# Output projection with features, not heads, on the column tiles, and a new memory made by cast and 32x32 transpose

## The chip, the cores and the metric

The kernel runs on one core of a Trainium2 chip. The metric is the device time of one execution in microseconds. The core has five engines that run side by side and wait for each other through semaphores: TensorE (PE, with its weight loads shown as PEld), VectorE (DVE), ScalarE (ACT), GpSimd (POOL) and SyncE (SP, which issues transfers here). SBUF and PSUM have 128 partitions; TensorE writes its results to PSUM.

## The reference

Two results are mixed with a gate per token. `a` is attention with a recurrent memory: the sequence of 2048 tokens is cut into 64 segments of 32, each segment is put behind 8 memory rows, all 40 rows go through 32-head attention (mask, softmax, output projection Wo), the first 8 output rows become the memory of the next segment, the other 32 are output. `b` is layer norm, a two-layer MLP with gelu, and biases.

```python
for s in range(n_seg):                       # 64, one after the other
    h = concat([mem, x[:, 32*s:32*s+32]])    # 8 + 32 rows of 512
    q, k, v = h @ Wq, h @ Wk, h @ Wv         # 512 -> 32 heads x 128
    p = softmax(where(mask, q k^T * scale, -1e9))
    o = einsum('bhqk,bhke->bhqe', p, v)
    o = einsum('bhte,hed->btd', o, Wo)       # 32 heads x 128 -> 512
    mem = o[:, :8]                           # used by the next segment
    outs.append(o[:, 8:])
out = g * concat(outs) + (1 - g) * mlp(layernorm(x))
```

All inputs and the output are bf16.

## The kernel before, in words

The first 96 us are the MLP (its result goes to a DRAM buffer `c_dr`) with the loading of the attention weights; then comes the loop over 64 segments (`for s in range(nseg)`), about 10.2 us each, and a short end. The four segments `si` = 0 to 3 of a tile T of 128 tokens belong together. The order of all instructions is the order of the code (a manual schedule).

PE works with column tiles throughout: a matmul takes 128 rows (contraction), 32 columns of weights (32 query rows of the activations as weights) and a moving operand of up to 512 columns; `tile_position=(0, 32*c)` puts it on one of four column tiles, whose results land on partitions 32c to 32c+31. Four such matmuls, one per column tile, run at the same time; a group of four is called a set below. Each matmul has a weight load of its own.

The 40 rows of a segment are not computed together. 32 rows (24 of the new tokens and the 8 memory rows) go through the segment itself: `hT` holds them transposed (feature on the partition, 4 chunks `kc` of 128 features, 32 rows, of which the first RIDE=24 are tokens and the last 8 memory). The other 8 tokens of each of four segments (LEFT=8) are gathered into a 32-row group of the whole tile, and their projections do not depend on the memory. They are the fill: a generator `side(T, si)` gives 8 units of one set each (projections of the left rows of the next tile for si = 0, 1, 3; `wo_left`, the output projection of the left rows, for si = 2), and `run(n)` puts n units into PE's stream at chosen places. WS holds these numbers.

One segment in order: q and k (16 sets each of 512 columns, L122), transposes to QT and KT, scores in two halves (L259, L263), exp on ACT, v (L141), the sums (L270, L273, L616) and their reciprocals, `run(W1)`, attention times v (`av`: L283 and L288, two halves, the second of which needs the second normalization L710), casts to UT on ACT (L746), `run(W2)`, then the output projection.

`wo_pass` (function at L645) does the output projection of UT into the bank W. `wo_group` gives column tile c the heads i = 4*ih + c, so each column tile adds up other heads, over all 512 features; W then holds four partial sums, on partitions 32c + row. There are 8 sets of 512 columns. ACT casts W to `w` (L650, three pieces). `new_mem` (three calls) multiplies w with a selection matrix SelM (a 1 at 32c + m for each c), which adds up the four partial sums, transposes and picks the memory rows at once: 4 matmuls of 8 columns for a chunk of 128 features, 16 in all (L659). DVE casts the results to hT of the next segment (L661). A unit of fill stands between these steps. Only then can PE start q and k of the next segment.

The other output rows are picked in `out_sel` once per tile (L223, L227): SelR and SelL are matrices with a 1 for each of the four partial sums, again one set of 512 columns per matrix. In the loop it stands behind `wo_pass` of si = 0 (from T = 2 on). After the loop there are two more `wo_pass`, the rest of a `wo_left`, and the end (L805 to L818).

Of the kernel before, what the change touches and what calls it, by code (L numbers as in the profile page):

```python
# [27 lines left out]
def kernel(ctx, tc, A_x, A_mem0, A_Wq, A_Wk, A_Wv, A_Wo, A_seg_len, B_x, B_w1, B_b1, B_w2, B_b2, gate_w, out):  # L28
# [42 lines left out]
    hT = [ep.tile([P, KC, 32], BF16, name=f"hT{i}") for i in range(3)]  # L71
# [4 lines left out]
    MkF = ep.tile([P, 4 * EW + NG + 2 * M], BF16)  # L76
    Mk = MkF[:, 0:4 * EW].rearrange("p (a c) -> p a c", c=EW)
    BO = ep.tile([P, P], BF16)
    SelM = ep.tile([P, M], BF16)
    SelR = ep.tile([P, 32], BF16)  # L80
    SelL = ep.tile([P, P], BF16)
    SelI = ep.tile([P, 32], BF16)
# [36 lines left out]
    def qk_unit(bk, G, t, hf, kc):  # L119
        h0, h1 = HF[hf]  # L120
        for j in range(4):
            nc.tensor.matmul(bk[32 * j:32 * j + 32, :], lhsT=G[:, kc, :], rhs=W5[t][:, kc, h0:h1, j, :],  # L122
                             start=(kc == 0), stop=(kc == KC - 1), tile_position=(0, 32 * j))
# [15 lines left out]
    def v_unit(bk, G, vb, kc):  # L139
        for j in range(4):  # L140
            nc.tensor.matmul(bk[32 * j:32 * j + 32, :], lhsT=G[:, kc, :], rhs=Wv5[:, kc, 4 * vb:4 * vb + 4, j, :],  # L141
                             start=(kc == 0), stop=(kc == KC - 1), tile_position=(0, 32 * j))
# [4 lines left out]
    HORD = [(j, ih) for j in (0, 2, 1, 3) for ih in range(2)]  # L147

    def wo_group(bk, U_, n):
        j, ih = HORD[n]  # L150
        for c in range(4):
            i = 4 * ih + c
            nc.tensor.matmul(bk[32 * c:32 * c + 32, :], lhsT=U_[:, j, i, :], rhs=Wo_sb[:, 4 * i + j, :],  # L153
                             start=(n == 0), stop=(n == NW - 1), tile_position=(0, 32 * c))
# [53 lines left out]
    def wo_left(T, bk):  # L208
        for n in range(NW):
            wo_group(bk, UL[T % 2], n)  # L210
            if n < NW - 1:
                yield

        def ca():
            wl = cw.tile([P, Dm], BF16, tag="wl", name="wl")
            nc.scalar.copy(out=wl[:], in_=bk[:])
            wls[T] = wl
        act_q.append(ca)
        yield

    def out_sel(T, bk):
        for si in range(SPT):
            nc.tensor.matmul(bk[32 * si:32 * si + 32, :], lhsT=SelR[:], rhs=ws.pop(SPT * T + si)[:], start=True, stop=False,  # L223
                             skip_group_check=True, tile_position=(0, 32 * si))
        wl = wls.pop(T)
        for si in range(SPT):
            nc.tensor.matmul(bk[32 * si:32 * si + 32, :], lhsT=SelL[:, 32 * si:32 * si + 32], rhs=wl[:], start=False, stop=True,  # L227
                             skip_group_check=True, tile_position=(0, 32 * si))

        def ev():  # L230
            o = cw.tile([P, Dm], BF16, tag="o", name="o")
            nc.vector.scalar_tensor_tensor(out=o[:], in0=bk[:], scalar=g_all[:, T:T + 1], in1=cs.pop(T)[:], op0=ALU.mult, op1=ALU.add)
            nc.sync.dma_start(out2[T * P:(T + 1) * P, :], o[:])
        dve_q.append(ev)
        yield
# [14 lines left out]
    def mask_put(i2):  # L250
        c = 4 * EW + (NG + 2 * M if i2 == 0 else 0)
        nc.vector.tensor_copy(out=(SbF, W)[i2][:, 0:c], in_=MkF[:, 0:c])
# [41 lines left out]
    with tc.tile_pool(name="mlpw", bufs=1) as mlpw, \  # L294
# [72 lines left out]
        nc.gpsimd.memset(SelM[:], 0.0)  # L367
        nc.gpsimd.memset(SelR[:], 0.0)
        nc.gpsimd.memset(SelL[:], 0.0)
        nc.gpsimd.memset(SelI[:], 0.0)  # L370
        for c in range(4):
            nc.gpsimd.affine_select(out=SelM[:], in_=SelM[:], pattern=[[-1, M]], compare_op=ALU.not_equal, fill=1.0, base=-32 * c, channel_multiplier=1)
            for q0, a, b in ((0, RIDE, 32), (LEFT, 0, RIDE)):
                nc.gpsimd.affine_select(out=SelI[:, a:b], in_=SelI[:, a:b], pattern=[[-1, b - a]], compare_op=ALU.not_equal, fill=1.0, base=-32 * c - q0, channel_multiplier=1)
            nc.gpsimd.affine_select(out=SelR[:, 0:RIDE], in_=SelR[:, 0:RIDE], pattern=[[-1, RIDE]], compare_op=ALU.not_equal, fill=1.0, base=-32 * c - M, channel_multiplier=1)
            nc.gpsimd.affine_select(out=SelL[:].rearrange("p (s t) -> p s t", s=SPT)[:, :, RIDE:seg], in_=SelL[:].rearrange("p (s t) -> p s t", s=SPT)[:, :, RIDE:seg],
                                    pattern=[[-LEFT, SPT], [-1, LEFT]], compare_op=ALU.not_equal, fill=1.0, base=-32 * c, channel_multiplier=1)
# [231 lines left out]
    xs8z = SbF[:, 4 * EW + NG:4 * EW + NG + 2 * M]  # L609
# [35 lines left out]
    def wo_pass(U_, cuts=(0, Dm)):  # L645
        for n in range(NW):
            wo_group(W, U_, n)
        w = cw.tile([P, Dm], BF16, tag="w", bufs=8, name="w")
        for a, b in zip(cuts, cuts[1:]):
            nc.scalar.copy(out=w[:, a:b], in_=W[:, a:b])  # L650
        return w

    def new_mem(w, hn, n):

        k0, nk = ((0, 1), (1, 1), (2, 2))[n]
        bk = (U[1][:, 0:M], U[3][:, 0:M], xs8z)[n]
        for k in range(nk):
            for c in range(4):
                nc.tensor.matmul(bk[32 * c:32 * c + 32, M * k:M * k + M], lhsT=w[:, (k0 + k) * P + 32 * c:(k0 + k) * P + 32 * c + 32], rhs=SelM[:],  # L659
                                 start=n < 2, stop=True, skip_group_check=True, tile_position=(0, 32 * c))  # L660
        nc.vector.tensor_copy(out=hn[:, k0:k0 + nk, RIDE:32], in_=bk.rearrange("p (k m) -> p k m", k=nk))  # L661


    WS = ((2, 3, 0), (2, 2, 2), (2, 2, 2), (2, 2, 2))
    for s in range(nseg):
        T, si = divmod(s, SPT)
        last = s == nseg - 1
        hc, hn = hT[s % 3], hT[(s + 1) % 3]
        W1, W2, W3 = WS[si]
# [80 lines left out]
        w = wo_pass(UT[s % 2], (0, P, 2 * P, Dm))  # L750
        if s >= 1:
            ws[s - 1] = w
        run(W3)
        for _ in extra(T, si):
            pass
        new_mem(w, hn, 0)
        run(1)
        new_mem(w, hn, 1)
        run(1)
        new_mem(w, hn, 2)  # L760
# [38 lines left out]
    wf = wo_pass(UF, (0, Dm // 2, Dm))  # L799

    wl, c = wls.pop(T), cs.pop(T)
    halves = ((X1, slice(0, Dm // 2)), (X2, slice(Dm // 2, Dm)))
    for bk, cc in halves:
        for i in range(SPT):
            nc.tensor.matmul(bk[32 * i:32 * i + 32, cc], lhsT=SelL[:, 32 * i:32 * i + 32], rhs=wl[:, cc], start=True, stop=False,  # L805
                             skip_group_check=True, tile_position=(0, 32 * i))
        for i in range(si):
            nc.tensor.matmul(bk[32 * i:32 * i + 32, cc], lhsT=SelR[:], rhs=ws[SPT * T + i][:, cc], start=False, stop=True,
                             skip_group_check=True, tile_position=(0, 32 * i))
# [4 lines left out]
    for bk, cc in halves:  # L814
        nc.tensor.matmul(bk[32 * si:32 * si + 32, cc], lhsT=SelI[:], rhs=wf[:, cc], start=False, stop=True,
                         skip_group_check=True, tile_position=(0, 32 * si))
# [125 lines left out]
```

## Time and profile before

| what | value |
|---|---|
| time, median of 3 runs | 770.77 us (770.53 to 771.61) |
| span of the profiled execution, first to last instruction | 768.4 us |
| time of the profiled execution itself | not listed apart from the three runs; the median is 2.4 us above the span |
| busy PE, ACT, DVE, POOL | 753.4, 540.0, 396.1, 278.2 us |
| matmuls, each with a weight load | 19186 |
| output projection W (L153), matmuls | 2080, that is 65 passes of 32 |
| output projection of the left rows (L153, in X), matmuls | 512, that is 16 of 32 |
| new memory (L659), matmuls | 1008, that is 63 times 16 |
| ACT casts of W to w (L650) | 46.0 us |

How to read it: times are in microseconds unless marked ns. A row of the timeline gives start, length, engine, line, operation, result<-operands, shapes (partitions x elements) and how many instructions were merged (x4). The length of a row of matmuls runs to the end of the last one, whose time in the pipeline is part of it, so rows of PE overlap; the start of one row to the start of the next is the time that PE gave to the first. In the groups the numbers behind the bar are busy time, mean ns of one, idle time before and what ended it.

### The profile page before, as it was taken

To read this page: it belongs to the slowest core of one execution; us is meant where nothing else is said; L and a number is where in the kernel's file an instruction comes from. 1 tells how busy PE (TensorE), PEld (TensorE's weight loads), DVE (VectorE), ACT (ScalarE), POOL (GpSimd) and SP (SyncE) were. 2 spreads that over 40 slices of the span, in tenths; PEclk is the share of its full clock that TensorE was granted. 3 is DMA by queue.
4 is the path that set the end of the run, shared out by engine and by line. 5 is a ranking of instruction groups with operands and counts; after the bars stand their busy time and mean duration, and the time that the engine had idled before them with its cause. 6 is when DMAs were issued, how large, how long until landed. Compare 5 with 4: busy or idle time off the path is not lost.

```text
span 768.4 us, 43822 instructions
## 1 busy us (share of the span) xinstructions
PE 753.4 (98%) x19186; PEld 412.2 (54%) x19186; DVE 396.1 (52%) x1428; ACT 540.0 (70%) x1631; POOL 278.2 (36%) x522
## 2 busy tenths in 40 slices
PE   7999999999999999999999999999999999999996
PEld 5666554555555555555555555555555555555553
DVE  5776355445445454545554554545454555444444
ACT  4666676777777777777777777777777777777763
POOL 4111033433344443334434334443424443343341
PEclk9999999999999999999999999999999999999999
DMA  6779422223222222212131322122222213122221
GB/s 196 274 233 400 153 58 63 76 63 87 65 59 66 79 72 73 80 53 74 58 89 62 90 63 79 45 80 73 80 72 59 76 49 89 62 83 64 72 67 38
DMA packets 53319, 70.58 MB, mean 92 GB/s; under 512 B 21306, under 2 KB 43043, under 8 KB 51587
## 3 DMA queue, kind: packets, MB, share of 16 engines
q1 hardware_dynamic: 51394, 64.84, 26.8%
q8 instruction: 152, 2.49, 1.4%
q0 software_dynamic: 784, 1.97, 0.8%
q10 hardware_dynamic: 944, 0.92, 0.3%
q14 instruction: 45, 0.36, 0.2%
HBM read 56.96 MB, written 4.45 MB: 80 GB/s over the span
## 4 chain that ended last, share of the span: by engine, by line
PE 96%; DMA 1%; DVE 1%; ACT 1%; issue 0%; SPq 0%; POOL 0%; DVEq 0%; ACTq 0%
PE U L122 30%; PE X L141 18%; PE W L153 15%; PE X L122 7%; PE U L468 4%; PE U L283 4%; PE X L153 4%; PE W L462 2%; PE SbF L462 2%; PE U L270 1%; PE W L259 1%; DMA w_sb<-in_B_w_dram 1%; PE U L659 1%; PE SbF L259 1%; PE SbF L616 1%; PE U L288 1%
## 5 line engine op out<-in xcount | busy, mean ns | idle before, releaser
L643 POOL TENSOR_TENSOR UT<-XR,Rb 128x384 bf16<-128x384 bf16 x126 | 140.3, 1136 | 301.7 <-DMA Rb<-r_dr 220.5
L127 ACT CAST Tb<-U 128x512 bf16<-128x512 f32 x258 | 151.2, 586 | 78.4 <-PE U L122 78.1
L122 PEld LDWEIGHTS <-hT 128*32 128x32 bf16 x4096 | 104.5, 96 | 103.9 <-DVE hT L661 8.6
L141 PE MATMUL X<-Wv_sb,hT 128*32 128x512 bf16 x2048 | 143.8, 378 | 0.0
L122 PE MATMUL U<-Wq_sb,hT 128*32 128x512 bf16 x2048 | 136.1, 381 | 0.3 <-DVE hT L661 0.2
L122 PE MATMUL U<-Wk_sb,hT 128*32 128x512 bf16 x2048 | 132.7, 379 | 0.0
L153 PE MATMUL W<-Wo_sb,UT 128*32 128x512 bf16 x2080 | 124.6, 380 | 1.2 <-POOL racc L635 1.2
L661 DVE CAST hT<-U 128x8 bf16<-128x8 f32 x126 | 20.9, 167 | 172.8 <-PE U L659 163.6
L719 ACT CAST V<-X 128x256 bf16<-128x256 f32 x256 | 88.7, 372 | 14.5 <-PE X L141 0.8
L131 DVE STREAM_TRANSPOSE QT<-Tb 128x256 f32<-128x256 f32 x128 | 57.0, 446 | 76.5 <-ACT Tb L127 76.5
L153 PEld LDWEIGHTS <-UT 128*32 128x32 bf16 x2080 | 57.8, 96 | 56.5 <-issue 13.1
L650 ACT CAST w<-W 128x128 bf16<-128x128 f32 (+1 forms) x192 | 46.0, 311 | 48.2 <-PE W L153 48.2
L622 ACT CAST XR<-U 128x256 bf16<-128x256 f32 x252 | 78.4, 434 | 0.0
L131 DVE STREAM_TRANSPOSE KT<-Tb 128x256 f32<-128x256 f32 x128 | 57.0, 445 | 28.0 <-ACT Tb L127 23.5
L643 POOL TENSOR_TENSOR UL<-XR,Rb 128x128 bf16<-128x128 bf16 x126 | 60.3, 502 | 0.0
L141 PEld LDWEIGHTS <-hT 128*32 128x32 bf16 x2048 | 46.4, 94 | 21.0
L635 POOL TENSOR_TENSOR racc<-racc,R 128x72 f32<-128x72 f32 x63 | 21.3, 338 | 93.4 <-PE U L288 84.1
L468 PE MATMUL U<-w_sb,hTm 128*128 128x512 bf16 (+1 forms) x176 | 52.4, 381 | 0.0
L746 ACT CAST UT<-U 128x64 bf16<-128x64 f32 x252 | 35.4, 226 | 22.9 <-PE U L288 22.8
L462 PEld LDWEIGHTS <-w_sb 128*128 128x128 bf16 (+1 forms) x352 | 34.5, 102 | 20.1 <-issue 1.3
L702 ACT ACTIVATE E<-W 128x64 bf16<-128x64 f32 (+1 forms) x128 | 35.0, 273 | 11.3 <-PE W L263 11.3
L659 PEld LDWEIGHTS <-w 128*32 128x32 bf16 x1008 | 22.8, 93 | 37.2 <-ACT w L650 29.3
(159 smaller groups left out, 1204.7 us busy)
## 6 DMA issues: line engine op xcount, KB each, us to landing
Rb<-r_dr SPq DMA_DIRECT2D x63, 512.0 KB, 3.8
Wv_sb<-in_A_Wv_dram SPq DMA_DIRECT2D x4, 1024.0 KB, 6.3
Wq_sb<-in_A_Wq_dram SPq DMA_DIRECT2D x4, 1024.0 KB, 7.1
Wk_sb<-in_A_Wk_dram SPq DMA_DIRECT2D x4, 1024.0 KB, 9.4
Wo_sb<-in_A_Wo_dram SPq DMA_DIRECT2D x4, 1024.0 KB, 15.0
VP<-VL SPq DMA_DIRECT2D x64, 64.0 KB, 3.5
c<-c_dr SPq DMA_DIRECT2D x16, 128.0 KB, 3.6
xt<-in_A_x_dram SPq DMA_DIRECT2D x15, 128.0 KB, 3.1
```

The costliest lines, as they stand in the source:

```text
L122: nc.tensor.matmul(bk[32 * j:32 * j + 32, :], lhsT=G[:, kc, :], rhs=W5[t][:, kc, h0:h1, j, :], start=(kc == 0), stop=(kc == KC - 1), tile_ ...
L127: nc.scalar.copy(out=Tb[:], in_=bk.rearrange("p (a b e) -> p a e b", a=8, b=2))
L131: nc.vector.transpose(out=dst[:, 8 * hf:8 * hf + 8, c0:c0 + 32, :].rearrange("p a r b -> p a (r b)").bitcast(FP32), in_=Tb[:].rearrange("p ...
L141: nc.tensor.matmul(bk[32 * j:32 * j + 32, :], lhsT=G[:, kc, :], rhs=Wv5[:, kc, 4 * vb:4 * vb + 4, j, :], start=(kc == 0), stop=(kc == KC - ...
L153: nc.tensor.matmul(bk[32 * c:32 * c + 32, :], lhsT=U_[:, j, i, :], rhs=Wo_sb[:, 4 * i + j, :], start=(n == 0), stop=(n == NW - 1), tile_po ...
L462: nc.tensor.matmul(hp[:rows, 0:TB * P], lhsT=w1_sb[:, kc, fc * P:fc * P + rows], rhs=yTs[blk][:, kc, :], start=(kc == 0), stop=(kc == KC - 1))
L468: nc.tensor.matmul(bp(blk, tt)[:], lhsT=hTm[blk % 2][:rows, fc, tt * P:(tt + 1) * P], rhs=w2_sb[:rows, fc, :], start=(fc == 0), stop=(fc = ...
L622: nc.scalar.copy(out=XR[:, j], in_=U[j][:, 0:NG * 40].rearrange("p (i q) -> p i q", q=40)[:, :, 0:32])
L643: nc.gpsimd.tensor_tensor(out=out[:, :, 4 * h:4 * h + 4, o:o + b - a], in0=XR[:, :, 4 * h:4 * h + 4, a:b], in1=Rb[:, h, :, :, a:b], op=ALU ...
L650: nc.scalar.copy(out=w[:, a:b], in_=W[:, a:b])
L719: nc.scalar.copy(out=V[:, i0:i0 + 2, :].rearrange("p i e -> p (i e)"), in_=(X1, X2)[vb][:, 256 * h:256 * h + 256])
L746: nc.scalar.copy(out=UT[s % 2][:, j, :, 0:M], in_=U[j][:, 0:NG * 40].rearrange("p (i q) -> p i q", q=40)[:, :, 32:40])
```

## The change

Each column tile of `wo_group` computes other features instead of other heads. The view Wo4 cuts the 512 features into 4 blocks b of 128, each into 4 parts c of 32; column tile c takes part c of all blocks (128 columns) and adds up all 32 heads. So a pass has 32 sets of 128 columns instead of 8 sets of 512, with 128 matmuls and 128 weight loads instead of 32 and 32. W then holds finished sums in 128 columns: partition 32c + row, column 32b + f, feature 128b + 32c + f.

With that, a 32x32 block transpose on DVE gives the layout of hT directly. `wo_pass` with `hn` casts W to w on DVE in two halves of 64 columns, and transposes each half into hT (two chunks of 128 features each; hT grows to 56 columns, since a block brings 32 rows and only the 8 memory rows are used). `new_mem`, SelM and the casts on ACT go. `wl` and the two passes after the loop are still cast on ACT, in 128 columns.

`out_sel` and the end pick each part c apart: SelR, SelL and SelI hold one matrix per c, and the results go to strided columns (`by_col`). The 2 sets of 512 columns become 8 sets of 128. At the end, `half_mm` issues four matmuls of 64 columns in a row on the same column tile.

The fill is placed anew: WS was (W1, W2, W3), now (W1, W2). For si = 1 to 3 three units stand before `av` (two before), two before the output projection as before, and three behind it (four before). For si = 0 three stand before `av` (two before), three before the output projection as before, two behind it (three before).

```diff
     def wo_group(bk, U_, n):
         j, ih = HORD[n]
-        for c in range(4):
-            i = 4 * ih + c
-            nc.tensor.matmul(bk[32 * c:32 * c + 32, :], lhsT=U_[:, j, i, :], rhs=Wo_sb[:, 4 * i + j, :],
-                             start=(n == 0), stop=(n == NW - 1), tile_position=(0, 32 * c))
+        for i in range(4 * ih, 4 * ih + 4):
+            for c in range(4):
+                nc.tensor.matmul(bk[32 * c:32 * c + 32, 0:P], lhsT=U_[:, j, i, :], rhs=Wo4[:, 4 * i + j, c],
+                                 start=(n == 0 and i == 4 * ih), stop=(n == NW - 1 and i == 4 * ih + 3), tile_position=(0, 32 * c))
...
+    Wo4 = Wo_sb[:].rearrange("p h (b c f) -> p h c b f", b=KC, c=4)
+
+    def by_col(bk, si, c, b0=0, b1=KC):
+
+        return bk[32 * si:32 * si + 32, :].rearrange("p (b c f) -> p c b f", b=KC, c=4)[:, c, b0:b1]
...
     def out_sel(T, bk):
-        for si in range(SPT):
-            nc.tensor.matmul(bk[32 * si:32 * si + 32, :], lhsT=SelR[:], rhs=ws.pop(SPT * T + si)[:], start=True, stop=False,
-                             skip_group_check=True, tile_position=(0, 32 * si))
+        w4 = [ws.pop(SPT * T + si) for si in range(SPT)]
+        for c in range(4):
+            for si in range(SPT):
+                nc.tensor.matmul(by_col(bk, si, c), lhsT=SelR[:, c, :], rhs=w4[si][:].rearrange("p (b f) -> p b f", b=KC), start=(c == 0), stop=False,
+                                 skip_group_check=True, tile_position=(0, 32 * si))
...
-    def wo_pass(U_, cuts=(0, Dm)):
+    def wo_pass(U_, hn=None):
         for n in range(NW):
             wo_group(W, U_, n)
-        w = cw.tile([P, Dm], BF16, tag="w", bufs=8, name="w")
-        for a, b in zip(cuts, cuts[1:]):
-            nc.scalar.copy(out=w[:, a:b], in_=W[:, a:b])
+        w = cw.tile([P, P], BF16, tag="w", bufs=8, name="w")
+        for h in range(2):
+            c = slice(64 * h, 64 * h + 64)
+            if hn is None:
+                nc.scalar.copy(out=w[:, c], in_=W[:, c])
+            else:
+                nc.vector.tensor_copy(out=w[:, c], in_=W[:, c])
+                nc.vector.transpose(out=hn[:, 2 * h:2 * h + 2, RIDE:RIDE + 32], in_=w[:, c])
         return w
...
-    WS = ((2, 3, 0), (2, 2, 2), (2, 2, 2), (2, 2, 2))
+    WS = ((3, 3), (3, 2), (3, 2), (3, 2))
...
-        w = wo_pass(UT[s % 2], (0, P, 2 * P, Dm))
+        w = wo_pass(UT[s % 2], hn)
         if s >= 1:
             ws[s - 1] = w
-        run(W3)
         for _ in extra(T, si):
             pass
-        new_mem(w, hn, 0)
-        run(1)
-        new_mem(w, hn, 1)
-        run(1)
-        new_mem(w, hn, 2)
         for _ in fill:
             pass
...
+    def half_mm(bk, h, lhs, w, i, start, stop):
+        for c in range(4):
+            nc.tensor.matmul(by_col(bk, i, c, 2 * h, 2 * h + 2), lhsT=lhs(c), rhs=w[:, 64 * h:64 * h + 64].rearrange("p (b f) -> p b f", b=2),
+                             start=start and c == 0, stop=stop and c == 3, skip_group_check=True, tile_position=(0, 32 * i))
+
+    for bk, h in halves:
         for i in range(SPT):
-            nc.tensor.matmul(bk[32 * i:32 * i + 32, cc], lhsT=SelL[:, 32 * i:32 * i + 32], rhs=wl[:, cc], start=True, stop=False,
-                             skip_group_check=True, tile_position=(0, 32 * i))
+            half_mm(bk, h, lambda c: SelL[:, c, i, :], wl, i, True, False)
```

The selection matrices are set up by four POOL instructions instead of a loop of twenty, and the zero columns that `new_mem` needed in the mask (2M) go.

71 lines of the change are left out of this document (27 added, 44 removed).

## The prediction

> **What bounds the kernel now.** I read the spans first, then the busy shares and the chain that ended last, then two whole segments by windows, then the timeline of one segment.
>
> ```profile
> core 0: 768.4 us, clock 0.996
> PE 753.4 (98%) x19186; PEld 412.2 (54%) x19186; DVE 396.1 (52%) x1428; ACT 540.0 (70%) x1631; POOL 278.2 (36%) x522
> PE 96%; DMA 1%; DVE 1%; ACT 1%; issue 0%; SPq 0%; POOL 0%; DVEq 0%; ACTq 0%
> 406.59:416.82 10.23, 10.23 (x302) 5.43 (x296) 5.59 (x20) 7.52 (x24) 4.05 (x7) 1.00 0.11 32
> ```
>
> The chain is PE for 96% of the span, at the full granted clock. In the window (one segment: length, then busy PE, PEld, DVE, ACT, POOL) PE is busy without a break, while DVE works 5.6 and ACT 7.5 of 10.2 us. So what counts is PE's own streaming, and small losses that "busy" hides, because a matmul's drain is counted. These show in the starts:
>
> ```profile
> 402.77 0.30 PE L283 MATMUL U<-E,V 32*128 32x40 bf16 x16
> 402.89 0.21 PE L288 MATMUL U<-E,VP 32*128 32x64 bf16 x4
> 403.05 0.29 PE L283 MATMUL U<-E,V 32*128 32x40 bf16 x16
> 403.18 0.19 PE L288 MATMUL U<-E,VP 32*128 32x64 bf16 x4
> 403.31 0.61 PE L122 MATMUL X<-Wq_sb,GL 128*32 128x512 bf16 x8
> 403.77 1.91 PE L153 MATMUL W<-Wo_sb,UT 128*32 128x512 bf16 x32
> 405.49 0.62 PE L122 MATMUL X<-Wk_sb,GL 128*32 128x512 bf16 x8
> 406.04 0.19 PE L659 MATMUL U<-SelM,w 128*32 128x8 bf16 x4
> 406.08 0.39 PE L122 MATMUL X<-Wk_sb,GL 128*32 128x512 bf16 x4
> 406.30 0.18 PE L659 MATMUL U<-SelM,w 128*32 128x8 bf16 x4
> 406.32 0.39 PE L122 MATMUL X<-Wk_sb,GL 128*32 128x512 bf16 x4
> 406.54 0.20 PE L659 MATMUL SbF<-SelM,w 128*32 128x8 bf16 x8
> 406.59 1.11 PE L122 MATMUL U<-Wq_sb,hT 128*32 128x512 bf16 x16
> 407.52 1.04 PE L122 MATMUL U<-Wk_sb,hT 128*32 128x512 bf16 x16
> 409.25 1.04 PE L122 MATMUL U<-Wk_sb,hT 128*32 128x512 bf16 x16
> ```
>
> A set of 512 columns (four matmuls, one per column tile) takes (409.25 - 407.52) / 8 = 0.216 us. The eight sets of the output projection stream until 403.77 + 1.73 = 405.50. Then come four units of fill, 0.864 us, but q of the next segment starts only at 406.59, so 0.23 us are lost to the selection matmuls and to waiting for them, and q loses another 0.07 (1.11 against 1.04) because its later chunks of hT come late: 0.30 us a segment. The other loss lies between the two halves of attention times v: 0.16 us from 402.89 to 403.05.
>
> **The change part by part.**
>
> Passes. 8 sets of 512 columns become 32 sets of 128. No column-tiled set of 128 columns is in the trace. The nearest rows are four matmuls of 128 columns on the whole array, each with a weight load, and a column-tiled set of 64:
>
> ```profile
> 56.13 0.39 PE L441 MATMUL X<-ident,y 128*128 128x128 bf16 x4
> L441 PE MATMUL X<-ident,y 128*128 128x128 bf16 x64 | 6.2, 220 | 2.1 <-DVE y L434 1.9 <-DVE hT L493 0.2
> 399.99 0.20 PE L263 MATMUL SbF<-QT,KL 128*32 128x64 bf16 x4
> 400.02 1.25 PE L141 MATMUL X<-Wv_sb,hT 128*32 128x512 bf16 x20
> ```
>
> Four take 0.39 where one takes 0.22, so the step is 0.17 / 3 = 0.057; by columns, 0.030 for 64 and 0.216 for 512 give 0.057 too. All these are roundings of 0.01, and I take 0.056: 32 x 0.056 = 1.79 against 8 x 0.216 = 1.73, +0.064 a pass, over 65 + 16 = 81 passes +5.2 us. Each nanosecond more in a set costs 81 x 32 = 2.6 us. Bounds: 0.0545, and 0.070, since the two sets from 403.31 to 403.77 took 0.46 and not 0.432, 0.014 each beyond their streaming, which would be paid by every set if a weight load showed there.
>
> A rule speaks against this change. The Trainium skill, page "TensorE: Matmul & The Clock Gate", section "Back-to-back issue gap", states that a lasting stream of weight load and matmul pairs needs about 81 ns per matmul at 128 columns. By that the sum would be (81 - 56) x 2.6 = 65 us more, about 826. The trace disagrees as far as it goes: pairs at 0.057, if only four in a row, and the same section's figure of 131 ns for 512 columns is not what runs here either.
>
> `out_sel`: 2 sets of 0.216 become 8 of 0.056, +0.016, 15 times: +0.2 us.
>
> Fill ahead of `av`. One more unit stands before it. The second half of `av` waits for the normalization:
>
> ```profile
> 402.37 0.37 DVE L709 RECIPROCAL W<-U 128x32 f32<-128x32 f32 x1 [0.24 <-ACT E L702]
> 402.77 0.22 DVE L710 TENSOR_TENSOR E<-E,W 128x64 bf16<-128x64 bf16 x1
> ...
> 403.10 0.14 DVE L633 COPY R<-W 128x32 f32<-128x32 f32 x1
> ```
>
> L710 ends at 402.99, and 403.05 follows. Four matmuls of 64 columns need 0.03 of the 0.16, and 0.02 is spread in the first row (0.21 against 0.19), so 0.11 is wait. With `av` 0.216 later the wait is gone. What is queued behind `av` (UT casts, reciprocals, the transfer of Rb) moves with it by 0.1 us. 60 segments have fill there: -6.6 us. If nothing is gained, 0.
>
> Behind the pass. The four matmul groups of L659 and the three ACT casts go; two casts and two transposes on DVE come, with three units over them (0.648). DVE has nothing else there:
>
> ```profile
> 405.73 0.71 ACT L650 CAST w<-W 128x128 bf16<-128x128 f32 x3 [0.65 <-PE W L153]
> 406.35 0.44 DVE L661 CAST hT<-U 128x8 bf16<-128x8 f32 x2 [2.56 <-PE U L659]
> 406.85 0.17 DVE L661 CAST hT<-SbF 128x16 bf16<-128x16 f32 x1
> 406.94 0.22 DVE L766 TENSOR_TENSOR rmin<-rmin,R 128x72 f32<-128x72 f32 x1
> L661 DVE CAST hT<-U 128x8 bf16<-128x8 f32 x126 | 20.9, 167 | 172.8 <-PE U L659 163.6 <-PE SbF L659 3.2
> L661 DVE CAST hT<-SbF 128x16 bf16<-128x16 f32 x63 | 11.0, 175 | 3.8 <-PE SbF L659 0.3
> L131 DVE STREAM_TRANSPOSE KT<-Tb 128x256 f32<-128x256 f32 x128 | 57.0, 445 | 28.0 <-ACT Tb L127 23.5
> L137 DVE STREAM_TRANSPOSE KL<-Tb 128x128 f32<-128x128 f32 x64 | 20.4, 397 | 1.2 <-ACT Tb L127 1.2
> ```
>
> Casts of 8 and 16 columns differ by 8 ns, 1 ns a column, so one of 64 takes 167 + 56 = 0.223. No transpose of 64 bf16 columns is shown; the plain one of 256 takes 0.445, less 192 columns at 1 ns is 0.25 (chosen, as its access is the plain one; bounds 0.14, the short copy of 403.10, and 0.397, the strided KL row at its full length). From a matmul's end to the next engine I see 0.05 (405.68 to 405.73) and 0.12 (406.23 to 406.35) and take 0.08; between dependent DVE operations 0.03 (402.74 to 402.77); from a cast's end to PE 0.07 (406.52 to 406.59). The last set's results come 0.16 behind its streaming (0.22 - 0.056). So q can start 0.16 + 0.08 + 0.223 + 0.03 + 0.25 + 0.07 = 0.81 us after the streaming, 0.17 behind the three units. The second pair is some 0.42 later, as DVE starts the second cast while the transpose drains, and q's first two sets take 0.43: just in time. With 0.02 of restart that is 0.19 lost instead of 0.30; against the roundings I count 0.10. That holds for 45 segments of si = 1 to 3, -4.5 us. For si = 0 the rows are
>
> ```profile
> 434.65 1.90 PE L153 MATMUL W<-Wo_sb,UT 128*32 128x512 bf16 x32
> 437.68 0.82 PE L122 MATMUL U<-Wq_sb,hT 128*32 128x512 bf16 x12
> ```
>
> From 434.65 + 1.73 = 436.38 to 437.68 are 1.30 us with five sets (1.08), so 0.22 is lost; after, `out_sel` and two units (0.88) cover 0.81 and nothing is lost: 13 x 0.22 = -2.9. In the five segments with no or less fill the chain alone shortens, from 407.02 - 405.50 = 1.52 to 1.24: -1.4.
>
> The 46 us of casts that leave ACT, and the setup on POOL, I cost at nothing: both engines are behind PE. ACT comes to the next casts earlier, which nobody waits for.
>
> The end.
>
> ```profile
> 760.82 0.28 PE L805 MATMUL X<-wl,SelL 128*32 128x256 bf16 x4
> 761.46 0.54 PE L815 MATMUL X<-w,SelI 128*32 128x256 bf16 x2
> ```
>
> Selection takes 0.64 us, and half of it lay over ACT's cast. Four matmuls of 64 columns in a row on one column tile take 3 x 0.03 until the next tile can start: 14 x 0.09 = 1.27, and SelI 0.09: +0.7 us.
>
> Sum: 5.2 + 0.2 - 6.6 - 4.5 - 2.9 - 1.4 + 0.7 = -9.3 us. The span of 768.4 becomes 759.1; the median of the runs is 2.4 above the span, and I keep that: 761.5.
>
> **The rivals.**
>
> Slower by the weight loads. If a column tile's weights can't be loaded while its 0.053 us of streaming run, every set pays the 0.014 above: 2592 x 0.014 = +36, 798 us. The point from which it decides is 9.3 / 2.6 = 3.6 ns: at 0.0596 a set, nothing is gained. For it: the only proof of 0.056 has four in a row. Against it: sets of 64 columns keep 0.03. The Trainium skill's 81 ns is this rival at a higher price.
>
> Slower by the chain on DVE. At 0.397 a transpose, q starts at 0.96 and its third set at about 1.56 instead of 1.25: 0.31 in 63 segments but less where si = 0 has cover, +18, 779 us. It decides from about 0.33 a transpose.
>
> Slower by code. The pass issues 256 PE instructions in 1.8 us instead of 64.
>
> ```profile
> q8 instruction: 152, 2.49, 1.4%
> ```
>
> The row gives packets, MB and share of the 16 transfer engines. 2.49 MB over the 38372 matmuls and weight loads is 65 bytes each, so a packet of 16 KB holds about 250 of them and takes 0.014 x 16 x 768 / 152 = 1.1 us. One packet per pass fits if it is asked for ahead; if half a microsecond shows in each of 65 passes, 794 us. Against it: `av` runs 80 (40 matmuls with their loads) in the 0.54 us from 402.77 to 403.31, and its one gap is the wait named above.
>
> Faster still: with transposes of 0.14 the 0.19 goes to 0.02, -8 us, 753.
>
> **How the numbers follow.** Forecast 0.50 (own range 755 to 768), faster still 0.16, DVE's chain 0.12, with 0.04 between it and the forecast that ends within 0.2%, weight loads 0.13, code 0.05. Of the 0.13, the price of the Trainium skill's page holds 0.02. 0.2% (1.5 us) is about what a measurement of this kernel can tell from no change. Faster 0.66, same 0.04, slower 0.30. The range leaves out the weight loads and the code, 0.18: from 750 (fast transposes and sets of 0.0545) to 780.
>
> **What would show it.** Right: rows W<-Wo_sb,UT 128x128 x128 that stretch over 1.79 us of starts; no gap over 0.03 between the halves of `av`; q's first row about 0.81 us behind the streaming; about 10.1 us a segment for si = 1 to 3 and 10.4 for si = 0. Wrong: passes of 2 us or more (weight loads), holes inside a pass ended by issue (code), transposes over 0.33 or a cast that starts late behind another DVE operation.

## The result, and the profile after

The changed kernel takes 948.46 us (median of 4 runs, 944.89 to 955.15) beside 770.65 us before (770.25 to 771.61): a ratio of 1.2312, 95% interval 1.2283 to 1.2341. The prediction was 761.5. The loss is 178 us.

The changed kernel's span, its busy times (column x: instructions), the chain that ended last, and its row of instruction packets:

```profile
core 0: 943.1 us, clock 0.977
PE 781.4 (83%) x26362; PEld 506.2 (54%) x26362; DVE 424.2 (45%) x1491; ACT 492.8 (52%) x1443; POOL 274.5 (29%) x505
PE 81%; issue 16%; DVE 1%; ACT 1%; DMA 1%; POOL 0%; DVEq 0%; POOLq 0%; ACTq 0%
q8 instruction: 208, 3.41, 1.5%
```

PE's share of the chain fell from 96% to 81%, and 16% is now "issue": time in which PE waited for no semaphore that the profile shows. Its instructions, matmuls and weight loads together, rose from 38372 to 52724, and the packets of queue q8 from 152 to 208. At 256 instructions to a packet these are 38912 and 53248, so q8 is taken as the queue that brings PE its instructions. No engine took the chain over.

The rows for PE in the list of waits of the same kernel (total us, times, longest) say where:

```profile
PEld L157 <- issue: 117.2, 100, 3.9
...
PE W L157 <- issue: 68.2, 55, 3.5
PEld L121 <- issue: 47.4, 84, 2.2
```

L157 is the output projection, L121 is q and k right behind it. Matmul and load rows overlap, so they are not added. I went through the starts of PE's records instead: 116 places in the loop where nothing starts for over 0.45 us, 177.5 us in all, 1.53 us each. In the kernel before, the same count gives 8 places and 4.8 us. So the holes bring 172.7 us of the 174.7 between the two spans; that nothing seems to be left over is partly chance, as shown below. In the changed kernel most of these places lie 255 or 256 records apart, or 511, 512 or 767. Two stretches from one resumption to the next, by windows (length, then busy time and count of PE, PEld, DVE, ACT, POOL, then granted clock, share and GB/s of the transfer engines):

```profile
438.37:441.84 3.47, 3.11 (x128) 1.90 (x128) 2.02 (x6) 2.56 (x8) 1.31 (x3) 1.00 0.02 7
441.84:445.39 3.55, 1.89 (x129) 1.64 (x129) 0.76 (x4) 1.67 (x8) 0.91 (x3) 1.00 0.04 6
```

128 matmuls and 128 loads, then 129 and 129 (the border falls within a rounding of a record): one packet of 256 instructions each, and some 3.5 us for each. In the second PE is busy for 1.89 us and then dry. The timeline around it shows the hole in the middle of a pass, ended by nothing but the next packet:

```profile
443.15 0.57 PE L157 MATMUL W<-Wo_sb,UT 128*32 128x128 bf16 x28
445.39 2.47 PEld L157 LDWEIGHTS <-UT 128*32 128x32 bf16 x100 [1.84 <-issue]
445.39 2.74 PE L157 MATMUL W<-Wo_sb,UT 128*32 128x128 bf16 x100 [1.66 <-issue]
```

Across the 116 places PE starts again a median of 1.41 us after an instruction packet has landed (5 to 95%: 1.21 to 1.59).

The packets' starts follow PE, too. With the borders between packets placed by the holes, a packet in the loop starts a median of 1.14 us after PE has begun on the packet before it (middle half 1.04 to 1.62). Then 1.04 us on its way (median) and 1.41 until PE starts make 3.6 us, about what the two stretches above took. So one packet is on its way ahead of PE, not several, and 256 instructions take about 3.5 us even where PE could work them off sooner. That PE's entry into a packet sets off the next one is inferred from these times; no record shows the request.

The starved kernel pays a second time. Its granted clock is at half in ten stretches of the loop, 37.5 us in all; the kernel before has none there. In one of them, four sets of 512 columns take 867.54 - 865.83 = 1.71 us, 0.43 each instead of 0.216:

```profile
865.83 1.93 PE L121 MATMUL U<-Wk_sb,hT 128*32 128x512 bf16 x16
867.54 1.68 PE L121 MATMUL U<-Wq_sb,hT 128*32 128x512 bf16 x16
865.45:868.85 3.40, 3.40 (x40) 1.35 (x36) 1.11 (x3) 1.17 (x2) 0.05 (x1) 0.50 0.00 0
```

Each of the ten begins at most 5.2 us after the start of a hole of 1.88 us or more; e2_split2 and e9_split_v below, whose holes stay under 1.6 us, have none in their loops. 37.5 us at half are some 19 us lost. So 172.7 us of holes and 19 of clock stand against 174.7 between the spans, and the rest of the change must have gained some 17 us (an estimate, the remainder of these numbers).

Outside the holes and these stretches the changed kernel does nearly what the prediction said. One pass with its surroundings (start, length of the row, engine; DVE's rows after PE's):

```profile
506.73 0.27 PE L290 MATMUL U<-E,V 32*128 32x40 bf16 x16
506.84 0.19 PE L295 MATMUL U<-E,VP 32*128 32x64 bf16 x4
506.87 0.29 PE L290 MATMUL U<-E,V 32*128 32x40 bf16 x16
...
507.61 1.17 PE L157 MATMUL W<-Wo_sb,UT 128*32 128x128 bf16 x69
510.08 1.02 PE L157 MATMUL W<-Wo_sb,UT 128*32 128x128 bf16 x59 [1.31 <-issue]
510.88 0.86 PE L140 MATMUL X<-Wv_sb,GL 128*32 128x512 bf16 x12
511.14 0.22 DVE L654 CAST w<-W 128x64 bf16<-128x64 f32 x1 [3.41 <-PE W L157]
511.40 0.25 DVE L655 STREAM_TRANSPOSE hT<-w 128x64 bf16<-128x64 bf16 x1
511.57 0.18 DVE L654 CAST w<-W 128x64 bf16<-128x64 f32 x1
511.70 1.05 PE L121 MATMUL U<-Wq_sb,hT 128*32 128x512 bf16 x16
511.79 0.24 DVE L655 STREAM_TRANSPOSE hT<-w 128x64 bf16<-128x64 bf16 x1
```

The pass is 69 matmuls, a hole, and 59 matmuls. Its groups on DVE:

```profile
L655 DVE STREAM_TRANSPOSE hT<-w 128x64 bf16<-128x64 bf16 x126 | 31.0, 246 | 4.4
L654 DVE CAST w<-W 128x64 bf16<-128x64 f32 x126 | 25.8, 205 | 217.3 <-PE W L157 217.3
```

### The profile page after: what moved, and what is told of

Read it like the earlier page. It is cut to its first block, busy times and chain, and to the rows that moved or that the text cites. A ratio compares the mean times of both kernels' runs of the same rounds, so it can differ in the third digit from the quotient of the medians.

```text
span 943.1 us, 57822 instructions
## 1 busy us (share of the span) xinstructions
PE 781.4 (83%) x26362; PEld 506.2 (54%) x26362; DVE 424.2 (45%) x1491; ACT 492.8 (52%) x1443; POOL 274.5 (29%) x505
## 4 chain that ended last, share of the span: by engine, by line
PE 81%; issue 16%; DVE 1%; ACT 1%; DMA 1%; POOL 0%; DVEq 0%; POOLq 0%; ACTq 0%
PE U L121 26%; PE X L140 15%; PE W L157 14%; PE X L121 6%; PE U L469 4%; PE X L157 4%; PE U L290 2%; PE W L463 2%; PE SbF L463 2%; PE U L277 1%; PE SbF L266 1%; PE W L266 1%; PE SbF L616 1%; PE U L295 1%; DMA b1r<-in_B_b_dram 1%
## 5 line engine op out<-in xcount | busy, mean ns | idle before, releaser
L157 PE MATMUL W<-Wo_sb,UT 128*32 128x128 bf16 x8320 | 143.9, 222 | 71.0 <-issue 68.2
L121 PEld LDWEIGHTS <-hT 128*32 128x32 bf16 x4096 | 119.6, 100 | 141.5 <-issue 41.0
L157 PEld LDWEIGHTS <-UT 128*32 128x32 bf16 x8320 | 125.4, 98 | 92.4 <-issue 85.9
L121 PE MATMUL U<-Wq_sb,hT 128*32 128x512 bf16 x2048 | 150.4, 398 | 12.8 <-issue 11.1
L121 PE MATMUL U<-Wk_sb,hT 128*32 128x512 bf16 x2048 | 146.2, 387 | 6.5 <-issue 5.4
L654 DVE CAST w<-W 128x64 bf16<-128x64 f32 x126 | 25.8, 205 | 217.3 <-PE W L157 217.3
L126 ACT CAST Tb<-X 128x512 bf16<-128x512 f32 x62 | 39.1, 631 | 81.4 <-PE X L121 81.4
L157 PE MATMUL X<-Wo_sb,UL 128*32 128x128 bf16 x2048 | 43.1, 229 | 28.8 <-issue 28.8
L140 PEld LDWEIGHTS <-hT 128*32 128x32 bf16 x2048 | 55.1, 94 | 14.2
L643 POOL TENSOR_TENSOR UL<-XR,Rb 128x128 bf16<-128x128 bf16 x126 | 60.4, 502 | 0.0
L157 PEld LDWEIGHTS <-UL 128*32 128x32 bf16 x2048 | 34.2, 101 | 33.8 <-issue 31.3
L220 ACT CAST wl<-X 128x128 bf16<-128x128 f32 x16 | 4.3, 266 | 86.0 <-PE X L157 86.0
```

Of the source, the lines that this page charges most:

```text
L121: nc.tensor.matmul(bk[32 * j:32 * j + 32, :], lhsT=G[:, kc], rhs=W5[t][:, kc, h0:h1, j, :], start=(kc == 0), stop=(kc == KC - 1), tile_pos ...
L126: nc.scalar.copy(out=Tb[:], in_=bk.rearrange("p (a b e) -> p a e b", a=8, b=2))
L140: nc.tensor.matmul(bk[32 * j:32 * j + 32, :], lhsT=G[:, kc], rhs=Wv5[:, kc, 4 * vb:4 * vb + 4, j, :], start=(kc == 0), stop=(kc == KC - 1) ...
L157: nc.tensor.matmul(bk[32 * c:32 * c + 32, 0:P], lhsT=U_[:, j, i, :], rhs=Wo4[:, 4 * i + j, c], start=(n == 0 and i == 4 * ih), stop=(n == ...
L643: nc.gpsimd.tensor_tensor(out=out[:, :, 4 * h:4 * h + 4, o:o + b - a], in0=XR[:, :, 4 * h:4 * h + 4, a:b], in1=Rb[:, h, :, :, a:b], op=ALU ...
L654: nc.vector.tensor_copy(out=w[:, c], in_=W[:, c])
```

## The experiments

The theory from these profiles: PE is limited by the rate at which its instructions arrive. The rivals: the new layout of the passes or the chain over DVE costs the time, or a single thick place in the program, or a transfer that gets in the way of the packets.

A row that returns below is a window over the loop alone, without start and end. From it I work out a rate, matmuls plus loads per us. For the kernel before, and then the changed one:

```profile
130.00:740.00 610.00, 607.22 (x17025) 322.88 (x17020) 306.31 (x1100) 446.05 (x1397) 242.14 (x427) 1.00 0.24 70
```

```profile
130.00:900.00 770.00, 633.83 (x23480) 408.65 (x23480) 334.21 (x1161) 403.42 (x1221) 241.16 (x427) 0.98 0.19 57
```

34045 / 610 = 55.8 per us before, with PE never dry; 46960 / 770 = 61.0 after, with PE dry for 177.5 us.

**Only more instructions, four times and twice (e1_split4, e2_split2).** The kernel before, with each 512-column matmul of `wo_group` cut into four of 128 or two of 256 columns. Heads, selection, ACT's casts and fill stay as they were.

```
-        for c in range(4):
-            i = 4 * ih + c
-            nc.tensor.matmul(bk[32 * c:32 * c + 32, :], lhsT=U_[:, j, i, :], rhs=Wo_sb[:, 4 * i + j, :],
-                             start=(n == 0), stop=(n == NW - 1), tile_position=(0, 32 * c))
+        for q in range(0, Dm, 128):      # e2_split2: steps and widths of 256
+            for c in range(4):
+                i = 4 * ih + c
+                nc.tensor.matmul(bk[32 * c:32 * c + 32, q:q + 128], lhsT=U_[:, j, i, :], rhs=Wo_sb[:, 4 * i + j, q:q + 128],
+                                 start=(n == 0 and q == 0), stop=(n == NW - 1), skip_group_check=True, tile_position=(0, 32 * c))
```

> The kernel before; each matmul of 512 columns in the output projection (wo_group) is cut into four of 128 columns, each with its own weight load. Same sums in W, same ACT casts, same selection matmuls for the new memory: the pass has the 128 matmuls of the changed kernel, and nothing else of the change. Theory 1 (TensorE's instructions don't arrive in time; only their number counts): the gaps of 1.5 us come back, about as slow as the changed kernel or a little slower, 930 to 970 us. Theory 2 (the gaps come from the new chain over VectorE and the new fill, not from the number): 81 passes x 0.06 us more than before, about 776 us.

> The same with two matmuls of 256 columns: 64 matmuls a pass, 640 instead of 576 TensorE instructions in a plain segment. Theory 1: if instructions come at one packet (256) in about 3.5 us, 640 need 8.8 us of the 10.2 of a segment, so only some gaps, 775 to 810 us; if the loss goes with the number of instructions alone, a third of that of four cuts, about 830. Theory 2: 772 us.

Measured: e1_split4 985.03 us (973.56 to 993.71, above the 970 that I gave as the upper end), ratio 1.2771 (1.2657 to 1.2885); e2_split2 803.95 us, ratio 1.0432 (1.0383 to 1.0482). The chain, the packets and the loop's window of e1_split4:

```profile
PE 80%; issue 15%; DVE 2%; ACT 1%; DMA 1%; POOL 0%; DVEq 0%; ACTq 0%; POOLq 0%
q8 instruction: 212, 3.47, 1.5%
130.00:930.00 800.00, 661.81 (x24184) 413.24 (x24184) 315.33 (x1102) 449.02 (x1409) 241.23 (x430) 0.97 0.19 55
```

and of e2_split2:

```profile
PE 94%; issue 3%; DVE 1%; ACT 1%; DMA 0%; POOL 0%; DVEq 0%; ACTq 0%
q8 instruction: 172, 2.82, 1.5%
130.00:770.00 640.00, 619.18 (x19315) 384.44 (x19311) 306.76 (x1097) 445.45 (x1395) 242.20 (x427) 1.00 0.22 67
```

Cutting the matmuls alone, with nothing else of the change, costs more than the whole change. Holes of over 0.45 us: 111 with 175.1 us, and 50 with 34.1 us. The rates are 60.5 and 60.4 per us, beside 61.0 of the changed kernel. So the new layout of features, the DVE chain and the order of the fill are not the cause; the number of instructions in the pass is. From 172 to 212 packets the spans go from 802.3 to 971.8 us, 4.24 us a packet, and 256 / 4.24 is 60.4 per us again. In part that is luck: e1_split4 has 55 us at half clock in its loop, some 27 of the 169.5 us, and e2_split2 none.

**The change without its instructions (e3_wide, e8_wide_ws).** The changed kernel with the eight sets of 512 columns of before in `wo_group`; casts, transposes and fill are the changed kernel's. The sum over the four groups of heads is left out, and with it three quarters of the features that are used, so this is no complete projection. e8_wide_ws also puts the fill back to where it was before.

```
-        for i in range(4 * ih, 4 * ih + 4):
-            for c in range(4):
-                nc.tensor.matmul(bk[32 * c:32 * c + 32, 0:P], lhsT=U_[:, j, i, :], rhs=Wo4[:, 4 * i + j, c],
-                                 start=(n == 0 and i == 4 * ih), stop=(n == NW - 1 and i == 4 * ih + 3), tile_position=(0, 32 * c))
+        for c in range(4):
+            i = 4 * ih + c
+            nc.tensor.matmul(bk[32 * c:32 * c + 32, :], lhsT=U_[:, j, i, :], rhs=Wo_sb[:, 4 * i + j, :],
+                             start=(n == 0), stop=(n == NW - 1), tile_position=(0, 32 * c))
...
-    WS = ((3, 3), (3, 2), (3, 2), (3, 2))          (e8_wide_ws only)
+    WS = ((2, 3), (2, 2), (2, 2), (2, 2))
```

> The changed kernel, but wo_group is the old one (8 sets of 512 columns, each column tile its own heads); casts, transposes and selection read the first 128 columns of W as in the changed kernel. Left out: the sum over the four head groups and three quarters of the features, so the new memory has other values. Theory 1: no gaps, and the terms of the prediction without the 5.2 us of the passes hold: 751 to 760 us, about 756. Theory 2: as slow as the changed kernel, 930 to 950 us.

> The wide version (no gaps) with the fill placed as in the kernel before: two units before attention times v, four (three for si = 0) behind the pass. The wait of 0.11 us in attention times v comes back in 60 segments (+6.6 us); the wait of 0.12 us behind the pass goes in 45 (-5.4): 751 to 756 us, about 754. Then the shorter chain is the gain and the place of the fill hardly matters. If the place of the fill were the gain, 765 or more.

Measured: 752.53 us, ratio 0.9762 (0.9737 to 0.9787), and 753.43 us, ratio 0.9759 (0.974 to 0.9778). The pass of e3_wide in the timeline, and its loop's window:

```profile
406.01 1.91 PE L157 MATMUL W<-Wo_sb,UT 128*32 128x512 bf16 x32
407.73 0.83 PE L157 MATMUL X<-Wo_sb,UL 128*32 128x512 bf16 x12
407.97 0.22 DVE L654 CAST w<-W 128x64 bf16<-128x64 f32 x1 [1.84 <-PE W L157]
408.23 0.24 DVE L655 STREAM_TRANSPOSE hT<-w 128x64 bf16<-128x64 bf16 x1
408.39 0.18 DVE L654 CAST w<-W 128x64 bf16<-128x64 f32 x1
408.52 1.05 PE L121 MATMUL U<-Wq_sb,hT 128*32 128x512 bf16 x16
```

```profile
130.00:720.00 590.00, 587.60 (x16348) 310.84 (x16340) 322.87 (x1153) 401.36 (x1218) 241.45 (x426) 1.00 0.24 72
```

With 55.4 instructions per us the same chain over DVE makes the kernel faster by 19 us (771.57, the kernel before in the same rounds, - 752.53). q starts 0.79 us behind the end of the streaming at 407.73. The two kernels hardly differ, so the place of the fill is worth about nothing here. That leaves the shorter chain, with the selection matmuls gone from PE, as the gain; no run takes the two apart.

**Part of the instructions (e4_mixed).** The changed kernel with `wo_left` and the selection by `SelL` in the form of before, the passes of every segment as changed.

```
+    def wo_group_l(bk, U_, n):                      (the wo_group of before)
...
-            wo_group(bk, UL[T % 2], n)
+            wo_group_l(bk, UL[T % 2], n)
...
-        for c in range(4):
-            for si in range(SPT):
-                nc.tensor.matmul(by_col(bk, si, c), lhsT=SelL[:, c, si, :], rhs=wl[:].rearrange("p (b f) -> p b f", b=KC), start=False, stop=True,
-                                 skip_group_check=True, tile_position=(0, 32 * si))
+        for si in range(SPT):
+            nc.tensor.matmul(bk[32 * si:32 * si + 32, :], lhsT=SelL[:, 32 * si:32 * si + 32], rhs=wl[:], start=False, stop=True,
+                             skip_group_check=True, tile_position=(0, 32 * si))
```

> The changed kernel, but the output projection of the left rows (wo_left, in segments with si = 2) and its selection are in the old form: 192 TensorE instructions fewer in 15 segments, 24 fewer in the selection of a tile. The passes of all segments keep their 32 sets of 128. Theory 1: the segments with si = 2 fall from 15.2 us to those of si = 1 and 3, about 12: 15 x 3.2 = 48 us less, 890 to 910. Theory 2: only streaming changes, 945 us.

Measured: 885.13 us, somewhat below the 890 to 910 of the theory, ratio 1.1454 (1.1415 to 1.1492). Its packets and its loop:

```profile
q8 instruction: 193, 3.16, 1.5%
130.00:840.00 710.00, 612.64 (x21569) 375.16 (x21560) 327.46 (x1139) 401.07 (x1202) 237.59 (x420) 0.99 0.20 60
```

60.8 per us: the same rate with fewer instructions. Fifteen packets less than the changed kernel, and a span shorter by 943.1 - 883.7 = 59.4 us, 4.0 us each.

**The same number in another place (e9_split_v).** The kernel before, with the 512-column matmuls of v cut in two instead of those of the output projection.

```
-        for j in range(4):
-            nc.tensor.matmul(bk[32 * j:32 * j + 32, :], lhsT=G[:, kc, :], rhs=Wv5[:, kc, 4 * vb:4 * vb + 4, j, :],
-                             start=(kc == 0), stop=(kc == KC - 1), tile_position=(0, 32 * j))
+        for q in (0, 2):
+            for j in range(4):
+                nc.tensor.matmul(bk[32 * j:32 * j + 32, 128 * q:128 * q + 256], lhsT=G[:, kc, :], rhs=Wv5[:, kc, 4 * vb + q:4 * vb + q + 2, j, :],
+                                 start=(kc == 0 and q == 0), stop=(kc == KC - 1), skip_group_check=True, tile_position=(0, 32 * j))
```

> The kernel before with every 512-column matmul of v (line 141, X<-Wv_sb,hT and X<-Wv_sb,GL, 2560 of them) cut into two of 256 columns: as many more instructions on TensorE as e2_split2 adds, but in another place, in the 0.9 us sets of v instead of the output projection. Theory that the number of instructions over the loop decides, 256 to a packet and one packet in about 4.2 us at best (from 172 to 212 packets the profiled spans went from 802.3 to 971.8 us, 4.24 us each): 170 to 174 instruction packets, and 795 to 812 us, as e2_split2. Rival theory that the thick place in the output projection decides (1024 instructions of PE in a row there): 771 to 778 us, since the plain segment would still have no place thicker than 72 instructions per us for longer than 1.2 us. Rival that cutting a matmul costs by itself (about 0.056 us more per set of four): 2560/4 sets by at most 0.06 us, up to 809 us, but with no idle time named 'issue' and gaps no more than before's 5 us.

Measured: 815.75 us, ratio 1.0601 (1.055 to 1.0653).

```profile
PE 92%; issue 4%; DVE 1%; ACT 1%; DMA 0%; POOL 0%; DVEq 0%; POOLq 0%; ACTq 0%
q8 instruction: 172, 2.82, 1.5%
130.00:780.00 650.00, 616.82 (x19396) 386.15 (x19392) 307.63 (x1098) 447.22 (x1398) 241.99 (x427) 1.00 0.22 66
```

172 packets again, 59.7 per us, 54 holes with 46.8 us. It ends 4 us above the upper end that I gave. The rival of the thick place in the output projection (771 to 778) is out, and cutting as such is out too, because the time shows as "issue". But the place does count: 5120 instructions more cost 46 us here (815.75 - 769.88), and 5184 cost 32 us in the output projection (803.95 - 771.57), with 46.8 and 34.1 us of holes. A mean rate can't tell these two apart; the 3.5 us of a packet can, in direction. An estimate from the trace of before: its PE starts, with the matmuls in question doubled and cut into packets of 256 that last 3.5 us at least, grow by 47 us for v, by 21 for the output projection, and by 8 with nothing doubled. So v's place fits, and a part of e2_split2's holes stays open.

**The transfer beside the packets (e5_no_rb, e10_rb_twice).** The 512 KB transfer into `Rb` once a segment is the only large one in the loop. e5_no_rb takes it away and uses a constant, which leaves out the normalization of the 24 rows that it is for; e10_rb_twice issues it a second time into a tile that nobody reads.

```
-        Rb = cw.tile([P, P, NG], FP32, tag="Rb", bufs=1, name="Rb")          (e5_no_rb)
-        nc.sync.dma_start(r_dr[s % 2][:], R[:, 8 * NG:RW])
-        nc.sync.dma_start(Rb[:].rearrange("p r e -> p (r e)"), r_dr[s % 2][:].rearrange("r e -> (r e)").partition_broadcast(P))
...
-        Rbs[s] = Rb
+        Rbs[s] = RbC
...
+        nc.sync.dma_start(RbX[:].rearrange("p r e -> p (r e)"), r_dr[s % 2][:].rearrange("r e -> (r e)").partition_broadcast(P))   (e10_rb_twice)
```

> The changed kernel without the two transfers that carry the reciprocals of a segment to all partitions (r_dr and Rb, 512 KB broadcast); a constant stands in Rb. Left out: the normalization of the 24 ridden rows with their own sums. Theory 1a (the instruction transfers are slow by themselves): as slow as the changed kernel, 935 to 960 us. Theory 1b (they wait behind the large Rb transfer on the transfer engines): most gaps go, below 850 us.

> The changed kernel with the 512 KB transfer into Rb issued a second time, into a tile that nobody reads, right behind the first on SP's queue. e5_no_rb took the transfer away and the profiled span went from 943.1 to 884.4 us. Theory that the instruction packets are held up by the packets of this transfer: another 25 to 65 us, 970 to 1010 us, with the same 208 instruction packets. Rival theory that e5_no_rb was faster because GpSimd's products waited for nothing (304.5 us of idle time there went) and the packets have nothing to do with it: 945 to 955 us, no change.

Measured: e5_no_rb 887.68 us, ratio 1.1499 (1.1467 to 1.1531); e10_rb_twice 958.66 us, ratio 1.2471 (1.2424 to 1.2518). The chain and the loop of e5_no_rb, then the loop of e10_rb_twice:

```profile
PE 84%; issue 12%; DVE 1%; DMA 1%; ACT 1%; POOL 0%; SPq 0%; DVEq 0%; POOLq 0%; ACTq 0%
130.00:840.00 710.00, 612.13 (x23232) 397.14 (x23228) 329.11 (x1148) 400.17 (x1208) 235.58 (x420) 0.99 0.07 18
```

```profile
130.00:900.00 770.00, 633.08 (x23159) 408.12 (x23163) 330.26 (x1146) 397.44 (x1202) 236.53 (x420) 0.97 0.31 96
```

Both fell between their theories. Without the transfer 65.4 instructions arrive per us instead of 61.0, and 130.8 us of holes stay of 177.5; with it doubled 60.2. So the transfer slows the packets, by about 7%, but it isn't what starves PE, and a second one adds only about 10 us more. What changes is when a packet starts: a quarter of them later than 1.62 us after PE's entry into the packet before in the changed kernel, later than 1.16 without the transfer; the time on the way does not fall with it (medians 1.04 and 1.12). A part of both results is the clock: 10 us at half in e5_no_rb's loop instead of 37.5, and 51 in e10_rb_twice, whose holes hardly grew (179.1 us). Counted over the packets of the changed kernel, those between whose starts more than 256 KB of other data moved came 4.55 us apart (76), the others 3.95 (123), which fits. Why the second transfer costs so much less than the first stays open.

**Two other ways to the gain (e6_assist, e7_fill).** Both start from the kernel before. In e6_assist DVE takes the second and fourth of four casts of `w`, and one fill unit between the selections goes; in e7_fill only the fill moves, as in the change.

```
-        for a, b in zip(cuts, cuts[1:]):                                                      (e6_assist)
-            nc.scalar.copy(out=w[:, a:b], in_=W[:, a:b])
+        for k, (a, b) in enumerate(zip(cuts, cuts[1:])):
+            (nc.scalar.copy if k % 2 == 0 else nc.vector.tensor_copy)(out=w[:, a:b], in_=W[:, a:b])
...
-        w = wo_pass(UT[s % 2], (0, P, 2 * P, Dm))
+        w = wo_pass(UT[s % 2], (0, P, 2 * P, 3 * P, Dm))
...
-    WS = ((2, 3, 0), (2, 2, 2), (2, 2, 2), (2, 2, 2))                                        (e7_fill)
+    WS = ((3, 3, 0), (3, 2, 1), (3, 2, 1), (3, 2, 1))
```

> The kernel before, with VectorE taking the second and fourth of four casts of W to w (it idles there 2.6 us), and the first two selections for the new memory next to each other. No more instructions on TensorE. hT's second chunk comes about 0.17 us earlier, the third about 0.1; q loses 0.05 us less a segment: 766 to 770 us, about 768; a gain would be the first version faster than the kernel before with all of its work done. If the casts were not on the path, 771.

> The kernel before with the changed kernel's placing of the fill alone: three units before attention times v instead of two, one behind the pass less. The wait of 0.11 us between the halves of attention times v goes, but the old chain (ACT casts, selection, VectorE casts) keeps its length and has 0.216 us less to cover it: 45 x (0.216 - 0.11) = +4.8 us and 15 x -0.05: about 775 us (772 to 778). If the fill's place alone were the gain of the wide version, 764.

Measured: e6_assist 807.48 us, ratio 1.0461 (1.0444 to 1.0478), a clear miss; e7_fill 774.19 us, ratio 1.0030 (1.0017 to 1.0043). In e6_assist's timeline the four casts stand one behind the other:

```profile
411.82 0.27 ACT L650 CAST w<-W 128x128 bf16<-128x128 f32 x1 [0.92 <-PE W L153]
412.11 0.29 DVE L650 CAST w<-W 128x128 bf16<-128x128 f32 x1 [2.51 <-ACT w L650]
412.44 0.27 ACT L650 CAST w<-W 128x128 bf16<-128x128 f32 x1 [0.36 <-DVE w L650]
412.74 0.29 DVE L650 CAST w<-W 128x128 bf16<-128x128 f32 x1 [0.33 <-ACT w L650]
```

Each waits for the other engine's cast: 1.21 us from 411.82 to 413.03, where ACT alone needed 0.71 in the kernel before. The Trainium skill, page "PSUM — Partial Sum Buffer", section "PSUM bank collisions raise a hardware error", says that the compiler's scheduler makes any two instructions of different engines that touch the same bank and quadrant wait for each other, reads too. These rows agree; that the tile `w`, which both write, orders them instead, no run here excludes. e7_fill shows that the moved fill alone doesn't gain here.

No run here points to a complete kernel that beats the one before: e3_wide is the faster form, but it leaves the sum over the head groups out.

## Why the prediction was wrong

The step that failed is the term for the instructions' arrival. The sum has none, as "One packet per pass fits if it is asked for ahead", and the rival "Slower by code", which names the mechanism, had its price and its chance (0.05) far off. It was sized at half a microsecond a pass, +33 us. Measured were 177.5 us of holes, 2.7 us for each of the 65 passes and the segment around it.

The mistake was to look at one pass: 256 instructions, one packet of 1.1 us, which "fits if it is asked for ahead". It is asked for ahead, but by one packet: PE can work off the 256 instructions of a pass in 1.8 us, but can start on the next 256 only some 3.5 us after it started on these. And the mean was near the limit before the change. The row 406.59:416.82 that the prediction itself quotes holds 302 + 296 = 598 instructions in 10.23 us, 58.5 per us. The change adds 192 to a pass and takes 32 of selection away: 758, over the forecast 10.1 us, 75 per us. The packets were taken to follow each other every 1.1 us, the time that one is on its way. In the trace of before they start no closer than 3.1 us apart, and only 5% of them closer than 3.4: 256 / 3.4 = 75 per us is thus what one packet in twenty reached there. The forecast needed that rate all the time. Over the loop, with its dense and its sparse packets, it is 60 to 61 (e1, e2, e4 and the changed kernel), and the kernel before ran at 55.8, 8% under it. A share of 1.4% of the transfer engines made this queue look idle. The argument against the rival, 80 instructions in 0.54 us within `av`, shows only that PE can take what has already arrived.

The Trainium skill bears on just this: its page "Runtime: NRT & Kernel Launch", section "Instruction fetch mechanics", has instructions come in blocks of 16 KiB, 256 instructions, fetched while the engine works on what it has, with the cost of crossing a block mostly hidden. The blocks of 256 agree with the holes' distance, and the fetching of the next during the current one with the 1.14 us; "mostly hidden" holds for the kernel before (4.8 us) and not for this change (177.5 us).

The other steps, one by one:

- Passes. 69 matmuls from 507.61 take 1.17 us; less the 0.22 of the last one these are 17 sets in 0.95, 0.056 each, as taken. The rival "Slower by the weight loads" (0.070) is out, and with it the 81 ns for 128 columns of the Trainium skill, page "TensorE: Matmul & The Clock Gate", section "Back-to-back issue gap", which the page gives per matmul and the prediction took per set: where instructions are there, neither shows.
- Fill ahead of `av`. The second half follows the first by 0.03 (506.84 to 506.87); the wait is gone. That it would give 6.6 us is not borne out: e7_fill moves the fill alone and is 0.3% slower, and e8_wide_ws without it is as fast as e3_wide.
- Behind the pass. From the end of the streaming at 510.88 to q at 511.70 are 0.82 us, predicted 0.81. The transposes take 0.246 (taken: 0.25), the casts 0.205 (taken: 0.223). "Slower by the chain on DVE" is out. Three units of 0.216 cover 0.65, and 0.17 is lost, as worked out.
- The sum without the passes and without instructions running short: -6.6 - 4.5 - 2.9 - 1.4 = -15.4. e3_wide, which has just that, gains 19.0 (771.57 - 752.53). Its parts are shared out differently than I had them, since nothing of it hangs on the fill, so the nearness of the two sums is partly luck.
- The clock. The prediction kept the full granted clock; behind the holes it stood at half for 37.5 us, some 19 us that no rival had.
- `out_sel` (+0.2) and the end (+0.7) can't be seen apart beside the rest.

What would make the prediction wrong was named too, "holes inside a pass ended by issue (code)", and this is what the rows at 445.39 and 510.08 show.

## What to carry to other kernels

Before cutting a matmul into narrower ones, count the engine's instructions per microsecond over the loop, matmuls and weight loads together, and compare with what the trace shows it to get when it runs dry (here 60 to 61 per us over the loop). Busy time doesn't show how near that limit is, and the share of the instruction queue doesn't either; the distance between instruction packets does. Then count over each 256 instructions in a row: here a stretch whose work was shorter than about 3.5 us waited for the next packet. So equal numbers of added instructions cost 46 us in one place and 32 in another.

## What the runs showed of the hardware

- Over the loop, starved PE worked off about 60 to 61 instructions per us in variants of this kernel (changed 61.0, e1_split4 60.5, e2_split2 60.4, e4_mixed 60.8, e10_rb_twice 60.2; e9_split_v 59.7), and at 65.4 without the 512 KB transfer once a segment.
- A starved PE got 256 instructions in about 3.5 us (438.37 to 441.84 to 445.39): a packet starts 1.14 us after PE has begun on the one before, is on its way for 1.04 us, and PE starts 1.41 us after it has landed (medians). What fills the 1.14 and the 1.41 us, no run here shows.
- The granted clock was at half in stretches of 3.4 us behind holes of 1.88 us and more (changed kernel, 37.5 us in all), and a set of 512 columns took 0.43 us there.
- Sets of four 128-column matmuls in four column tiles, each with its own weight load, follow each other every 0.056 us as long as there are instructions.
- Casts of ACT and DVE that read the same accumulator bank and write the same tile ran one behind the other, 1.21 us for four (e6_assist); which of the two orders them stays open.
